# Attention, expert choice and feed-forward on one core: the first expert's number read at another place, and twelve products of the identity by itself

## The chip, the core and the metric

The kernel runs on one core of a Trainium2 chip. The metric is the device time of one launch in microseconds (us). Four engines compute: PE (TensorE, matrix products and transposes), DVE (VectorE), ACT (ScalarE) and POOL (GpSimd). SP (SyncE) issues most transfers, POOL the indirect ones that gather rows. All inputs and results are float32.

## What is computed

```python
def reference(**kwargs):
    attn_out = _attn_ref(q, k, v)                  # 2 x 12 heads, 448 tokens, head size 64, causal
    x = attn_out.transpose(0, 2, 1, 3).reshape(896, 768)
    x = _moe_ref(x, w_gate, w1, w2)
    return _moe2_ref(x, w_gate, w_val, w_out, rms_g)

def _moe_ref(x, w_gate, w1, w2):
    logits = x @ w_gate                            # 896 tokens, 8 experts, 112 tokens to each
    for idx in np.argsort(-logits.flatten()):      # greedy: best pair first
        tok, e = idx // E, idx % E
        if assigned[tok] >= 0 or counts[e] >= cap: continue
        assigned[tok] = e; counts[e] += 1
    for e in range(E):
        h = np.maximum(x[assigned == e] @ w1[e], 0.0)
        out[assigned == e] = h @ w2[e]
    return out

def _moe2_ref(x, w_gate, w_val, w_out, rms_g):
    xn = x / rms(x) * rms_g
    g = xn @ w_gate
    return silu(g) * (xn @ w_val) @ w_out
```

## The kernel before

It has three stages. Attention goes head by head and leaves its result in DRAM (`xs`, line 285) and the logits in `acc`. Then come eight rounds. In each, the fullest expert is found, the 112 tokens that it gets are named, their rows are gathered from `xs` into `xg`, and PE multiplies them with that expert's weights. The feed-forward stage follows.

The order of the work on PE, DVE, ACT and POOL is written out by hand, in strings of words that `emit` (line 710) turns into calls. A word with a prime belongs to the round before that of the same word without one. The string that the change touches is `START1`, which is run once, between attention and the first expert; in it a prime means round 0, no prime round 1, and a `+` work of the first expert. SP's order is not written out, it follows from the program.

Words of one round, as they stand in `START1`:

- `M`: the best logit of each token (`m`), which PE transposes into a row (`mr`, line 406) and ACT copies (`ms`, line 408).
- `G` and `P`: seven comparisons on DVE (`G`, lines 415 to 419; the second on POOL, all in four buffers in turn), and seven groups of seven small products on PE (`pc`, line 427: 8 columns each), which count for each token how many stand before it.
- `Q0`, `Q1`: the sums on PE (`ptot`, line 449), the choice of the expert on DVE (`kx`, line 476) and the tokens' places (`pos`, line 488).
- `Q2`: the expert's number as an integer (`eid`, line 492, one DVE instruction on one element), which SP reads into a register (line 493). The loads of the expert's 16 blocks of weights (`raw`, line 569, 384 KB each, on SP's queue) take their address from it.
- `O`, `F0`, `F1`: a table of places (line 497), seven products on PE (`pi`, line 505), the token numbers (`idx`, line 509), and the gather of 112 rows into `xg` (line 512, issued by POOL).
- `X0`, `X1`: PE transposes `xg` (`tp`, line 599), ACT copies it (`xf`, line 608). `U`, `D`: the expert's two products with the weights (`hp`, line 649, and `y`, line 663); the first `U` needs both copies and the first block of weights.

The `hp` sums lie in the accumulator banks of tag `c`, `cs` holds the identity (`ident`).

Of the kernel before, what the change touches and what calls it, by code (L numbers as in the profile page):

```python
# [24 lines left out]
F1 = 1024  # L25
# [11 lines left out]
SPLIT = 4  # L37
AHEAD = 18
START0 = 'M0 M1 G G'
START1 = "G1' G' P0' P1' G' P2' P3' P4' G' P5' G1' P6' Q0' Q1' M1 O' G F0' F1' G P0 P1 Q2' G G G P2 P3 G X0 P4 P5 G X1 P6 U0+ Q0 U1+ U2+ Q1 U3+ U4+ O"  # L40
ITER0 = "Y1 A0 M1 N2 U5 G F0' G U6 Q2' F1' U7 Y0 G G G D0 N1 P0 P1 A1 P2 D1 D2 D3 G P3 D4 G X0 D5 P4 P5 P6 N0 D6 Q0 X1 D7"
ITER = "U0 Q1' U1 N0 N1 N2 U2 U3 Q2' A0 M1 Y0 U4 O' Y1 G U5 F0' U6 F1' U7 A1 G D0 G P0 G P1 D1 D2 G P2 P3 G D3 D4 G D5 P4 P5 D6 P6 X0 D7 Q0 X1"
LASTR = "U0 C2 B4 U1 N0 N1 N2 I0 U2 U3 A0 Y0 Y1 U4 J2 B5 I1 U5 U6 C3 U7 D0 A1 J3 B6 D1 C4 B7 D2 D3 J4 C5 D4 J5 D5 C6 D6 D7 K0"
# [32 lines left out]
def tile_attn_moe_ffn(ctx, tc, qk, v, consts, wts, wgv, wout, rmsg, out):  # L76
    nc = tc.nc
# [9 lines left out]
    def banks(name, tag="c"):  # L87
        return pools["ps"].tile([128, 2, 512], F32, tag=tag, name=name, bufs=1)
# [4 lines left out]
    ident = cs[:, C_ID:C_ID + 128]  # L93
# [424 lines left out]
    def half64(src, j):  # L518
        return src[j // 4, j // 2 % 2, :, j % 2 * 384:j % 2 * 384 + 384]

    def load64(src):
        raw = ring.tile([128, 384, 2], U32, tag="raw", name="w64", bufs=NR)
        nc.sync.dma_start(out=raw, in_=src.bitcast(U32).rearrange("p (a b) -> p a b", b=2))
        return raw

    def widen(raw):
        g = cv.tile([128, 384], F32, tag="g64", name="g64", bufs=3)
        nc.scalar.activation(g, raw[:, :, 1].bitcast(F32), AF.Copy, scale=2.0 ** -112)  # L528
        gu = g.bitcast(U32)
        t = cv.tile([128, 384], U32, tag="t64", name="t64", bufs=3)  # L530
        x = t.bitcast(F32)
        nc.vector.tensor_scalar(t, gu, 3, None, op0=ALU.logical_shift_left)
        nc.vector.scalar_tensor_tensor(t, gu, 0x80000000, t, op0=ALU.bitwise_and, op1=ALU.bitwise_or)  # L533
        nc.vector.tensor_scalar(gu, t, 0xFF800000, None, op0=ALU.bitwise_and)
        nc.vector.scalar_tensor_tensor(g, raw[:, :, 0], 2.0 ** -52, g, op0=ALU.mult, op1=ALU.mult)  # L535
        nc.vector.tensor_add(x, x, g)  # L536
        return x

    def halves(x, hi, lo):
        nc.scalar.copy(hi, x)  # L540
        nc.vector.tensor_sub(lo, x, hi.bitcast(F32))
# [3 lines left out]
    def gate_val(half, which, dcs):  # L545
        c0 = half * S
        wh, wl = early[which]
        if (half, which) not in gv0:
            gv0[half, which] = bank("a" if half else "r", "pg")
        for dc in dcs:  # L550
            for n, (w, x) in enumerate(((wh, xnh), (wh, xnl), (wl, xnh))):
                nc.tensor.matmul(gv0[half, which][:, :S], w[:, dc * 128:dc * 128 + 128], x[:, dc, c0:c0 + S],  # L552
                                 start=(dc == 0 and n == 0), stop=(dc == 5 and n == 2))

    def tiles64():
        return (ring.tile([128, 768], F32R, tag="hi", name="hi", bufs=NH),
                ring.tile([128, 768], F32R, tag="lo", name="lo", bufs=NH))
# [135 lines left out]
    def turn_ids(c):  # L693
        if c == 0:
            nc.gpsimd.tensor_copy(idxf, idx)
            row = rt.tile([128, N], F32, tag="ms", name="ms", bufs=1)
            idrow.append(row[0:1])
            for half in range(2):
                pr = bank("r", "pr")
                for e in range(4):  # L700
                    nc.tensor.matmul(pr[0:1, e * CAP:e * CAP + CAP], idxf[:, 4 * half + e:4 * half + e + 1],
                                     ident[:CAP, :CAP], start=True, stop=True)
                nc.scalar.copy(idrow[0][:, half * 4 * CAP:(half + 1) * 4 * CAP], pr[0:1, :4 * CAP])
        else:
            pt = bank("r", "pt")
            for t in range(NT):
                nc.tensor.matmul(pt[:, t:t + 1], idrow[0][:, t * 128:t * 128 + 128], ones[0:1, 0:1], start=True, stop=True)
            nc.vector.tensor_copy(idt, pt[:, :NT])

    def emit(words, r0):  # L710
        for w in words.split():
            op, c, r = w[0], int(w[1:].rstrip("'+") or 0), r0 + w.count("+")
            if op in "MGPQ" or op in "OF":
                k = r + 2 - (w[-1] == "'")
                if 0 <= k < E:
                    getattr(rounds[k], op)(c)
            elif op == "K":
                half, which, part = c // 4, c // 2 % 2, c % 2
                gate_val(half, which, range(3 * part, 3 * part + 3))
            elif op == "S":  # L720
                sg0[c] = cv.tile([128, S], F32, tag="sg", name="sg", bufs=2)
                nc.scalar.activation(sg0[c], gv0[c, 0][:, :S], AF.Silu)
            elif op == "I":
                turn_ids(c)
            elif op == "B":
                raws64.append(load64(half64(wgv, c)))
            elif op == "C":
                wide.append(widen(raws64[c]))
            elif op == "J":
                if c % 2 == 0:  # L730
                    early.append(tiles64())
                hi, lo = early[c // 2]
                c0 = c % 2 * 384
                halves(wide[c], hi[:, c0:c0 + 384], lo[:, c0:c0 + 384])
            elif op == "X":
                if r + 1 < E:
                    if c == 0 and r >= 0:
                        exps.append(Expert(r + 1))
                    getattr(exps[r + 1], op)(c)
            elif op in "NY":  # L740
                if r > 0:
                    getattr(exps[r - 1], op)(c)
            else:
                getattr(exps[r], op)(c)

    ET = mybir.EngineType
    with tc.manual_schedule(engines={ET.PE, ET.Activation, ET.DVE, ET.Pool}):
        emit(START0, -2)
        emit(START1, -1)
        for r in range(E):  # L750
            emit(ITER0 if r == 0 else LASTR if r == E - 1 else ITER6 if r == E - 2 else ITER, r)
        emit(END, E)

    ectx.close()
    with ExitStack() as fctx:
# [13 lines left out]
        for fc in range(NFC):  # L769
            gh, gl = early[2 * fc] if fc < PRE else pair64(wgv[fc, 0])  # L770
            vh, vl = early[2 * fc + 1] if fc < PRE else pair64(wgv[fc, 1])
            for half in range(2):
# [3 lines left out]
                else:  # L776
                    pg = bank("a", "pg")
                    pv = bank("r", "pv")
                    for dst, wh, wl in ((pg, gh, gl), (pv, vh, vl)):
                        for dc in range(6):  # L780
                            for n, (w, x) in enumerate(((wh, xnh), (wh, xnl), (wl, xnh))):
                                nc.tensor.matmul(dst[:, :S], w[:, dc * 128:dc * 128 + 128], x[:, dc, c0:c0 + S],  # L782
                                                 start=(dc == 0 and n == 0), stop=(dc == 5 and n == 2))
# [112 lines left out]
```

## Time and profile before

| what | value |
|---|---|
| median of 3 runs | 613.68 us (613.35 to 613.87) |
| profiled execution, whole | 612.4 us |
| profiled execution, span from the first to the last instruction | 610.6 us |
| PE busy | 582.0 us, 95% of the span |
| DVE, ACT, POOL busy | 413.3, 231.3, 109.5 us |
| PE's share of the chain of work that ended last | 89% |
| gather `xg` and its share of that chain | 2% |
| mean clock granted to PE, of full speed | 0.976 |

The profile numbers its stretches in microseconds from the first instruction. Attention ends at about 119 us, the first `hp` product stands at about 141 us. A busy PE is one whose records cover the time; a granted clock of 1.00 is 2.4 GHz, 0.50 is 1.2 GHz.

### The profile page before, as it was taken

The page shows a single profiled execution, that of the slowest core. Times are in us where ns is not written, and L with a number is a line of the kernel's source. Part 1 is how long each engine was busy: PE and PEld are TensorE (multiplying, and loading weights), DVE is VectorE, ACT ScalarE, POOL GpSimd, SP SyncE. Part 2 cuts the span into 40 slices and gives each one's busy share as a digit, 9 for nine tenths or more (in the row PEclk, how much of TensorE's full clock was granted, in tenths as well). Part 3 has the DMA queues.
Part 4 walks back from the last instruction along what each step waited for, and adds up shares of the span by engine and source line. Part 5 has one row for each costly group of instructions (what it writes and reads, how often), then busy time and mean ns, then how long its engine had stood idle before and what let it go on. Part 6 is the DMA issues. An engine that isn't in the chain of part 4 may idle for free.

```text
span 610.6 us, 10757 instructions
## 1 busy us (share of the span) xinstructions
PE 582.0 (95%) x3814; PEld 518.9 (85%) x3814; DVE 413.3 (68%) x1176; ACT 231.3 (38%) x561; POOL 109.5 (18%) x102
## 2 busy tenths in 40 slices
PE   4899999758999999999999999999999999999995
PEld 3899999738697796877968799999999999999995
DVE  7799999695464454644364699999999972991400
ACT  5799999401031121120232444344343434331100
POOL 4677875130120201202000000000000000000210
PEclk9899999957999999999999999999999999999999
DMA  8988871109995958659794355445455530100210
GB/s 277 271 260 258 258 226 32 32 13 383 351 352 212 353 183 337 257 190 362 272 384 134 127 155 156 129 132 151 131 156 135 149 106 0 53 1 0 104 49 30
DMA packets 47973, 109.32 MB, mean 179 GB/s; under 512 B 15232, under 2 KB 17408, under 8 KB 47920
## 3 DMA queue, kind: packets, MB, share of 16 engines
q1 hardware_dynamic: 45280, 93.96, 47.2%
q0 software_dynamic: 2640, 14.68, 7.5%
q8 instruction: 30, 0.49, 0.3%
q14 instruction: 23, 0.19, 0.1%
HBM read 103.12 MB, written 5.51 MB: 178 GB/s over the span
## 4 chain that ended last, share of the span: by engine, by line
PE 89%; DMA 5%; issue 2%; DVE 2%; SPq 1%; ACT 1%; POOL 1%; POOLq 0%; ACTq 0%; DVEq 0%
PE hp L649 14%; PE pv L782 13%; PE pg L782 13%; PE y L663 13%; PE o L803 12%; PE sp L178 4%; PE ot L237 4%; PE pt L207 4%; PE pn L264 3%; PE pg L552 2%; DMA xg<-xs,idx 2%; DMA cs<-in_consts 2%; PE tp L599 2%; PE pc L427 1%; PE mr L406 1%
## 5 line engine op out<-in xcount | busy, mean ns | idle before, releaser
L649 PE MATMUL hp<-xf,raw 128*128 128x112 f32 x768 | 92.3, 279 | 0.1
L649 PEld LDWEIGHTS hp<-xf,raw 128*128 128x128 f32 x768 | 89.4, 194 | 1.7 <-ACT hf L652 0.5
L663 PE MATMUL y<-raw,hf 128*112 128x384 f32 x256 | 89.4, 491 | 0.0
L663 PEld LDWEIGHTS y<-raw,hf 128*112 128x112 f32 x256 | 42.6, 177 | 27.4
L810 POOL DMA_INDIRECT out<-ob,idt x7 | 6.8, 969 | 296.2 <-ACT ob L809 290.5
L540 ACT CAST hi<-t 128x384 fp32r<-128x384 f32 x58 | 29.7, 512 | 58.4 <-DVE t L536 56.4
L199 ACT ACTIVATE pe<-sm,nm 128x256 f32<-128x256 f32 (+3 forms) x84 | 48.6, 582 | 2.5 <-DVE nm L189 2.1
L512 POOL DMA_INDIRECT xg<-xs,idx x8 | 21.5, 2684 | 155.3 <-DVE G L415 134.2
L782 PE MATMUL pv<-xnh,hi 128*128 128x448 f32 x132 | 48.2, 365 | 0.0
L782 PE MATMUL pv<-xnh,lo 128*128 128x448 f32 x132 | 48.2, 365 | 0.0
L782 PE MATMUL pv<-xnl,hi 128*128 128x448 f32 x132 | 48.2, 365 | 0.0
L782 PE MATMUL pg<-xnh,hi 128*128 128x448 f32 x132 | 48.2, 365 | 0.0
L782 PE MATMUL pg<-xnl,hi 128*128 128x448 f32 x132 | 48.2, 365 | 0.0
L782 PE MATMUL pg<-xnh,lo 128*128 128x448 f32 x132 | 48.2, 365 | 0.0
L189 DVE CUSTOM_DVE_ANT_0 sm<-sp,mask 128x384 f32<-128x384 f32 (+3 forms) x84 | 42.1, 514 | 2.9 <-PE sp L178 2.1
L207 PE MATMUL pt<-cs,pe 128*128 128x128 f32 x228 | 40.8, 286 | 3.3 <-DVE ptl L224 2.8
L224 DVE TENSOR_TENSOR ptl<-pt,pth 128x512 fp32r<-128x512 f32 (+3 forms) x84 | 41.4, 514 | 2.5 <-ACT pth L220 2.5
L528 ACT ACTIVATE g<-w 128x384 f32<-128x384 f32 x72 | 39.8, 554 | 5.7 <-DVE t L536 5.7
L220 ACT CAST pth<-pt 128x512 fp32r<-128x512 f32 (+3 forms) x84 | 37.1, 444 | 9.9 <-PE pt L207 8.0
L533 DVE SCALAR_TENSOR_TENSOR t<-g,t 128x384 uint32<-128x384 uint32 x72 | 39.1, 552 | 0.3
L536 DVE TENSOR_TENSOR t<-t,g 128x384 f32<-128x384 f32 x72 | 39.1, 552 | 0.3
L535 DVE SCALAR_TENSOR_TENSOR g<-w,g 128x384 f32<-128x384 uint32 x72 | 39.0, 552 | 0.3
(153 smaller groups left out, 1217.1 us busy)
## 6 DMA issues: line engine op xcount, KB each, us to landing
raw<-in_wts SPq DMA_DIRECT2D x128, 384.0 KB, 7.5
w<-in_wgv SPq DMA_DIRECT2D x48, 384.0 KB, 3.3
w<-in_wout SPq DMA_DIRECT2D x24, 384.0 KB, 3.2
hi<-in_qk POOLq DMA_DIRECT2D x10, 896.0 KB, 6.3
qr<-in_qk SPq DMA_DIRECT2D x11, 448.0 KB, 5.5
vr<-in_v SPq DMA_DIRECT2D x12, 224.0 KB, 4.6
xs<-xl SPq DMA_DIRECT2D x12, 224.0 KB, 3.8
kr<-in_qk SPq DMA_DIRECT2D x10, 224.0 KB
```

Source lines behind the costliest of these rows:

```text
L189: nc.vector.tensor_tensor_reduce(out=sm[:, :w], in0=sp[:, :w], in1=mask[:, MOFF[t]:MOFF[t] + w], op0=ALU.add, op1=ALU.min, scale=-0.125, s ...
L199: nc.scalar.activation(pe[:, :w], sm[:, :w], AF.Exp, bias=nm[:, t:t + 1], scale=-1.0, accum_out=sums[:, t:t + 1])
L207: nc.tensor.transpose(pt[:, b * 128:b * 128 + 128], pe[:, b * 128:b * 128 + 128], ident)
L224: nc.vector.tensor_sub(*rest.pop((h, t)))
L528: nc.scalar.activation(g, raw[:, :, 1].bitcast(F32), AF.Copy, scale=2.0 ** -112)
L533: nc.vector.scalar_tensor_tensor(t, gu, 0x80000000, t, op0=ALU.bitwise_and, op1=ALU.bitwise_or)
L535: nc.vector.scalar_tensor_tensor(g, raw[:, :, 0], 2.0 ** -52, g, op0=ALU.mult, op1=ALU.mult)
L536: nc.vector.tensor_add(x, x, g)
L649: nc.tensor.matmul(o, w[:, dc * 128:dc * 128 + 128], self.x[0][:, dc, :], start=(dc == 0), stop=(dc == 5))
L663: nc.tensor.matmul(self.ys[:CAP, u, :SQ], a, b[:, u * SQ:u * SQ + SQ], start=(c == 0 and i == 0), stop=(c == 7 and i == len(ps) - 1))
L782: nc.tensor.matmul(dst[:, :S], w[:, dc * 128:dc * 128 + 128], x[:, dc, c0:c0 + S], start=(dc == 0 and n == 0), stop=(dc == 5 and n == 2))
L803: nc.tensor.matmul(o[u][:, :SQ], x[:, fc % 6, :], w[:, u * SQ:u * SQ + SQ], start=(fc == 0 and n == 0), stop=(fc == NFC - 1 and n == 2))
```

## The change

In `START1` the word `Q2'` moves: it stood after the first two `P` of round 1, it now stands right after `Q1'`, ahead of `M1` and `O'`. New words `W1`, `W2`, `W2`, `W2`, `W5` stand after `F1'`, after the `P0`, `P1` and `P2` of round 1, and after `P3`, right ahead of the first `X0`. A word `Wn` multiplies the identity by itself n times (float32, 128 by 128 with 128 columns) into a bank of tag `c`; nothing reads the result.

```diff
-START1 = "G1' G' P0' P1' G' P2' P3' P4' G' P5' G1' P6' Q0' Q1' M1 O' G F0' F1' G P0 P1 Q2' G G G P2 P3 G X0 P4 ...
+START1 = "G1' G' P0' P1' G' P2' P3' P4' G' P5' G1' P6' Q0' Q1' Q2' M1 O' G F0' F1' W1 G P0 W2 P1 W2 G G G P2 W2 P3 W5 G X0 P4 ...
@@ emit
+            elif op == "W":
+                warm = banks("warm")[:, 0, :128]
+                for _ in range(c):
+                    nc.tensor.matmul(warm, ident, ident, start=True, stop=True)
```

On DVE, before: the row of the chosen expert's table (`oh`) and what follows it in round 0, up to the expert's number.

```order
L396 TENSOR_TENSOR oh<-ohf,km 128x56
L497 TENSOR_TENSOR O<-iota,pos 128x784
L499 SCALAR_TENSOR_TENSOR gone<-eo,gone 128x8
L416 SCALAR_TENSOR_TENSOR G<-ms,m,cs 128x128
L419 TENSOR_SCALAR G<-ms,m 128x768
L509 TENSOR_SCALAR idx<-pi 112x1
L415 TENSOR_SCALAR G<-ms,m 128x128
L416 SCALAR_TENSOR_TENSOR G<-ms,m,cs 128x128
L419 TENSOR_SCALAR G<-ms,m 128x640
L492 TENSOR_SCALAR eid<-kx 1x1
```

On DVE, now, the same stretch from the same row:

```order
L396 TENSOR_TENSOR oh<-ohf,km 128x56
L492 TENSOR_SCALAR eid<-kx 1x1
L497 TENSOR_TENSOR O<-iota,pos 128x784
L499 SCALAR_TENSOR_TENSOR gone<-eo,gone 128x8
L416 SCALAR_TENSOR_TENSOR G<-ms,m,cs 128x128
L419 TENSOR_SCALAR G<-ms,m 128x768
L509 TENSOR_SCALAR idx<-pi 112x1
```

The expert's number has moved ahead of eight instructions, among them `O` and `idx`, on which the gather rests. SP's order of instructions is the same in both kernels: the reading of the number stood, and stands, right ahead of the 16 loads.

On PE, before: the end of `P3` of round 1, then the transposes of the gathered rows, then `P4`.

```order
L427 LDWEIGHTS G
L427 MATMUL pc<-oh,G 128x8
L599 MATMUL tp<-cs,xg 128x112 x6
L427 LDWEIGHTS G
L427 MATMUL pc<-oh,G 128x8
```

On PE, now, the same place:

```order
L427 LDWEIGHTS G
L427 MATMUL pc<-oh,G 128x8
L726 MATMUL warm<-cs 128x128 x5
L599 MATMUL tp<-cs,xg 128x112 x6
L427 LDWEIGHTS G
```

Five of the twelve products stand between `P3` and the transposes that wait for the gather; the other seven stand one and two at a time between `pi`, `P0`, `P1`, `P2` and `P3`. Nothing else changes its place on any engine.

## Rows read from the trace of the kernel before

**Rows 1.** The page's 40 slices of 15.3 us: granted clock in tenths.

```profile
PEclk9899999957999999999999999999999999999999
```

**Rows 2.** Chain of work that ended last, 130 to 170: start us, us, what.

```profile
130.72 1.10 PE mr L406 x4
...
134.03 5.03 DMA xg<-xs,idx
...
139.10 1.38 PE tp L599 x6
140.48 0.54 PE pc L427 x21
141.02 2.74 PE hp L649 x12
143.76 0.43 PE ptot L449 x2
144.19 5.39 PE hp L649 x48
...
153.07 9.13 DMA xg<-xs,idx
...
162.25 0.80 PE tp L599 x6
...
164.34 0.51 PE pc L427 x21
...
166.23 0.21 PE ptot L449 x2
```

**Rows 3.** Busy us (and instructions) by stretch, then granted clock, DMA share, GB/s.

```profile
118.00:122.00 4.00, 1.59 (x16) 1.19 (x15) 3.20 (x13) 0.97 (x2) 1.75 (x3) 0.78 0.26 57
...
143.00:144.00 1.00, 1.00 (x7) 1.00 (x6) 0.00 (x0) 0.00 (x0) 0.00 (x0) 0.50 1.01 406
144.00:146.00 2.00, 2.00 (x19) 2.00 (x19) 1.60 (x12) 0.00 (x0) 0.00 (x0) 0.98 1.03 410
```

**Rows 4.** Timeline of DVE: start us, us, line, operation, tiles, shapes, count.

```profile
131.50 0.97 DVE L497 TENSOR_TENSOR O<-iota,pos 128x784 bf16<-128x784 bf16 x1
...
132.99 0.62 DVE L419 TENSOR_SCALAR G<-ms,m 128x768 bf16<-128x768 f32 x1
133.53 0.22 DVE L509 TENSOR_SCALAR idx<-pi 112x1 uint32<-112x1 f32 x1
...
134.58 0.13 DVE L492 TENSOR_SCALAR eid<-kx 1x1 uint32<-1x1 f32 x1
```

**Rows 5.** SP's timeline from 130 to 170: the loads of weights from their first issue.

```profile
135.80 31.47 SPq L569 DMA_DIRECT2D raw<-in_wts  x32
```

**Rows 6.** SP's waits, 118 to 170: who for whom, total us, times, longest.

```profile
SPq L493 <- DVE G L415: 16.2, 1, 16.2
```

**Rows 7.** Transfers issued from 135 to 136: count, size, us from issue to landing.

```profile
raw<-in_wts SPq DMA_DIRECT2D x1, 384.0 KB, 4.2
```

**Rows 8.** POOL's timeline at the first two gathers.

```profile
134.03 1.72 POOL L512 DMA_INDIRECT xg<-xs,idx  x1 [7.34 <-DVE G L415]
153.07 2.38 POOL L512 DMA_INDIRECT xg<-xs,idx  x1 [17.32 <-DVE G L415]
```

**Rows 9.** The eight gathers of `xg`: us from issue to landing.

```profile
DMA to landing us min/median/max: 5.0/9.3/10.5
```

**Rows 10.** Queues, 136 to 137 (q0 gathers; q1, weights, none): packets, MB, share.

```profile
q0 software_dynamic: 16, 0.10, 65.6%
```

**Rows 11.** The same queues, 137 to 138.

```profile
q0 software_dynamic: 57, 0.24, 65.2%
```

**Rows 12.** The same queues, 157 to 158; q0 has no line in it.

```profile
q1 hardware_dynamic: 129, 0.35, 92.8%
```

**Rows 13.** The same queues, 158 to 159.

```profile
q0 software_dynamic: 34, 0.21, 64.4%
```

**Rows 14.** Timeline of PE: eight of the small products of round 1.

```profile
134.72 0.76 PE L427 MATMUL pc<-oh,G 128*128 128x8 bf16 x8 [0.28 <-DVE eid L492]
```

More of the change, by code (lines that the diff above doesn't have):

```diff
@@ L39 @@
 START0 = 'M0 M1 G G'
-START1 = "G1' G' P0' P1' G' P2' P3' P4' G' P5' G1' P6' Q0' Q1' M1 O' G F0' F1' G P0 P1 Q2' G G G P2 P3 G X0 P4 P5 G X1 P6 U0+ Q0 U1+ U2+ Q1 U3+ U4+ O"
+START1 = "G1' G' P0' P1' G' P2' P3' P4' G' P5' G1' P6' Q0' Q1' Q2' M1 O' G F0' F1' W1 G P0 W2 P1 W2 G G G P2 W2 P3 W5 G X0 P4 P5 G X1 P6 U0+ Q0 U1+ U2+ Q1 U3+ U4+ O"
 ITER0 = "Y1 A0 M1 N2 U5 G F0' G U6 Q2' F1' U7 Y0 G G G D0 N1 P0 P1 A1 P2 D1 D2 D3 G P3 D4 G X0 D5 P4 P5 P6 N0 D6 Q0 X1 D7"
```

## The prediction

> **What bounds the kernel now.** The chain of waits comes first: PE holds 89% of it, and the page's clock line shows one lasting dip below full speed, in slices 9 and 10, between attention and the first expert [rows 1]. Nothing else in the kernel is near this change, so the whole sum is made there. Read next is the chain through that stretch [rows 2]. The first gather, issued at 134.03, takes 5.03 us; at 139.10 PE starts on its rows, and from there PE has no gap until the second gather. So the gather's landing sets the start of everything behind it, and PE's clock sets the pace. The stretches say what that pace is [rows 3]: the clock falls in 118 to 122, where PE was busy for 1.59 of 4 us, it is 0.50 (1.2 GHz) until 144, after PE has run without a gap from 139.10, and 0.98 (practically 2.4 GHz) from 144 to 146. The first expert therefore starts at half clock, and its start costs tp 1.38, pc 0.54, hp 2.74 and ptot 0.43, together 5.09 us, up to 144.19.
>
> The same work at the upper level stands in the same view [rows 2]: tp 0.80, pc 0.51, ptot 0.21, and a block of hp at 5.39 x 12/48 = 1.35, together 2.87 us. **If the clock were up when the gathered rows come, 2.22 us would be won; if the rows come later, each microsecond is lost whole.** With x for the rows' arrival and S for the time of that work (2.87 to 5.09), the shift against now is x + S - 144.19. Behind it PE is the bound; the second gather and the second expert's weights hang on PE's and DVE's work in this start and shift with it.
>
> **The expert's number.** The eid instruction takes 0.13 us at 134.58 and goes to the place of O at 131.50 [rows 4], 3.08 us earlier. O, pi and the gather's idx stand behind it, at most 0.13 us later. This is covered: idx waits behind G of line 419 in DVE's row, which runs from 132.99 when ACT's copy is there, and O, which would end at 132.6 instead of 132.47, leaves pi the time to be done at about 133.5, before idx at 133.53. Without that cover it would cost 0.13. SP waited 16.2 us for nothing but this number [rows 6], so its first load, 135.80 now [rows 5], goes out at 135.80 - 3.08 = 132.72; the 16 loads follow on the same queue, all 3.08 us earlier. Does PE gain from that? The first block lands 4.2 us after issue, at 140.0 [rows 7], and hp begins at 141.02: the weights had a second to spare, and the blocks behind it run ahead of a PE that has no gaps. With a faster start (hp at 139.10 + 0.80 + 0.51 = 140.4) they still would be there. So the earlier weights are worth nothing by themselves.
>
> **What they do to the gather.** POOL has the first gather written out at 134.03 + 1.72 = 135.75 [rows 8], just as SP issues its first load. In 136 to 137 only gather packets move (16), in 137 to 138 there are 57 more, 73 of the some 80 [rows 10, 11]: the gather has the engines nearly to itself, and lands 5.03 us after issue, the least of the eight; the median is 9.3, the largest 10.5 [rows 9]. With the change, SP has been issuing for 3.03 us when POOL is done. The nearest row is the second gather: issued at 153.07, written out at 155.45, in a time when SP issues the second expert's weights. Its packets do not show until 158, the weights' queue moves 129 packets from 157 to 158 and the gather's none, then 34 of its packets go from 158 to 159 [rows 12, 13], and it lands at 162.20, 9.13 us after issue [rows 2]. Taking off what POOL needed more there, 2.38 - 1.72, gives 8.47 us, and **x = 134.03 + 8.47 = 142.50** instead of 139.06. The ends: 5.03 us, if nothing changes (139.06), and the largest, 10.5 (144.5). I take 142.5, since the second gather is the one that also enters behind loads begun shortly before, while the weights of the first expert lie there longer still.
>
> The Trainium skill, page "DMA: Bandwidth & Descriptors", section "Queues, rings and completion order", says that each DMA engine takes turns between the queues that have work, a packet from each. The trace doesn't bear it out for the start of the second gather, which sees none of its packets moved while the weights' queue moves 129 [rows 12], but does from 158 on [rows 13]; by that rule the time would be rival B's, 613.5.
>
> **The twelve products.** A product of 128 columns in float32 is two passes, as each of hp's six is (12 records for one block). At half clock hp takes 2.74/12 = 0.228 us a pass for 112 columns, so 0.261 for 128, 0.52 a product, 6.3 us for twelve; at the upper level 1.35/12 = 0.112, so 0.26 a product. They stand on PE in order, and tp, P4 to P6 and hp queue behind the last five. From pi's end at about 133.4 to tp at 139.10 there are 5.7 us; the 28 small products of P0 to P3 take 28 x 0.76/8 = 2.7 [rows 14], which leaves 3.0 us empty. At half clock throughout, the products would end at 133.4 + 2.7 + 6.3 = 142.4; up to that much is on the path if the gather comes at 139.06, and nothing of it if it comes at 142.5. DVE's comparisons reuse four buffers that P0 to P2 free, up to a microsecond later than now; P4 to P6, which need the last ones, come after the gather, which covers it.
>
> Do they bring the clock up? The one rise here comes after 5.0 us in which PE had no gap, 139.10 to 144.1. With the products PE has none to speak of from 130.72 on (mr, pi, then products and counts) [rows 2]. If mr and pi count, the rise is at about 135.7, else about 138.4. The rest then goes at twice the pace as far as the comparisons allow, and the products end between 139.0 and 140.4 (middle 139.7). **After that PE stands empty again until 142.5**, some 2 to 3.5 us, and it is after such a thin stretch (1.59 busy of 4) that the clock fell before. So S is between 2.87 (still up) and 5.09 (fallen, or never up). Nothing in the trace favours one, and I take the middle, 3.98.
>
> **The sum.** 142.50 + 3.98 - 144.19 = +2.3 us, with +1.2 to +3.4 for the two ends of S. The profiled execution would go from 612.4 to 614.7; it lies 1.3 under the median of the runs, which goes from 613.68 to 616.0. What the measurement can tell from no change is 0.2%, 1.23 us.
>
> **Rivals.**
>
> A, the forecast: the weights hold the gather up for longer than the clock gives back. For it: the median of the eight gathers is 9.3 us, and the first is the only one that meets no weights when it is written out. 614.9 to 617.1, at the largest landing of a gather 617 to 619.
>
> B, turns between the queues. The gather's packets took about two microseconds alone, 136 to 138 [rows 10, 11]; shared one to one they would take as long again: x = 139.06 + 2.0 = 141.1, after the products end, with the clock up: 141.1 + 2.87 - 144.19 = -0.2, so 613.5, no change. Against it stands the second gather's late start; for it, that the weights' packets begin some two microseconds after the first issue (135.80, and none before 137 [rows 10]), so at about 134.7 with the change, which leaves them a lead of only one over the end of POOL's work.
>
> C, the other side: the gather is not touched, or barely, and the products' clock decides. Then tp waits for the last product, at 139.7, and S is 2.87: 139.7 + 2.87 - 144.19 = -1.6, so 612.1, faster, at best -2.3 (611.4). It decides if the rows are there before about 140.1. This is also what comes out if the loads don't go out earlier, because something that the trace covers holds SP, so that the first half of the change does nothing.
>
> D, the products do nothing for the clock and stand in front of tp: with the gather at 139.06, tp starts at 142.4 and S is 5.09, +3.3, so 617.0. For it: the counts between them have only 8 columns, and where PE did them alone the clock stayed down. Against it: the rise at 144 came with just such matrix work as the products are.
>
> **How the numbers follow.** A 0.58, B 0.19, C 0.16, D 0.07. The likeliest is A, 616.0. The range leaves out C's better half (0.08) and the top of A (0.07): 612.1 to 617.8; A's own range is 614.9 to 617.1. Slower by over 0.2%: A but for its lowest end (0.51) and D, 0.58. Faster by over 0.2%: C but for its weak end, and a B with a little more clock, 0.18. Within 0.2%: B and the edges, 0.24.
>
> **What would show it.** Right: the first load issued at about 132.7; the gather issued at 134.0 and landing at 141 to 143, with weights' packets and none of its own just after 135.75; PE empty between the last product and tp; the granted clock up somewhere in 135.7 to 140, and down again, or mixed, in 142 to 147. Wrong: a landing before 140.5 (then B or C), or a clock that holds at the upper level through the gap and a landing near 141, which brings the sum to zero; or PE coming to tp later than the rows (D). If the second gather is no longer met by PE just as it lands (162.20 against tp at 162.25), the shift does not pass on whole, which I have assumed.

## The result: slower, and by more than forecast

| | before | after |
|---|---|---|
| median of 5 runs | 613.75 us (613.35 to 614.93) | 621.5 us (620.94 to 622.99) |
| ratio, 95% interval | | 1.013 [1.0112, 1.0149] |
| profiled execution, whole | 612.4 us | 621.5 us |
| its span | 610.6 us | 619.7 us |
| mean clock granted to PE | 0.976 | 0.971 |

The change costs 7.75 us by the medians. The forecast was slower, 616.0, with a range up to 617.8: the direction was right, the size was not, and the range did not hold the time.

In the two profiled executions the spans differ by 9.1 us. 1.9 of this is no effect of the change: `mr`, the first step behind attention, starts at 132.61 here and started at 130.72 before [rows 2], and the five run times of each kernel spread by 1.58 and 2.05 us. To compare kernels I therefore count from the start of `mr`.

The page's clock line of after has its dip in the same place as [rows 1], and it is deeper:

```profile
PEclk9999999855999999999999999999999999999999
```

The chain of work that ended last, of after (start us, us, what), against [rows 2]:

```profile
132.61 1.09 PE mr L406 x4
...
135.92 12.42 DMA xg<-xs,idx
148.38 1.38 PE tp L599 x6
149.77 0.54 PE pc L427 x21
150.31 2.74 PE hp L649 x12
153.05 0.43 PE ptot L449 x2
153.47 5.46 PE hp L649 x48
...
171.54 0.58 PE tp L599 x6
```

The first gather now takes 12.42 us instead of 5.03, which is 7.39 more. `tp` starts 15.77 us after `mr` instead of 8.38, `hp`'s block of 48 20.86 instead of 13.47: both 7.39 later. `tp` of the second gathered rows starts 38.93 after `mr` instead of 31.53, 7.40 later. The work between `tp` and that block takes 5.09 us, as before. So the whole loss is the one gather's, and it passes on undiminished.

POOL's timeline of after, the first two gathers, against [rows 8]:

```profile
135.92 5.12 POOL L512 DMA_INDIRECT xg<-xs,idx  x1 [7.34 <-DVE G L415]
162.44 2.38 POOL L512 DMA_INDIRECT xg<-xs,idx  x1 [21.40 <-DVE G L415]
```

POOL needs 5.12 us to write out the first gather, against 1.72 before: 3.40 more. From POOL's end (141.04) to the landing (148.34) it is 7.30 us, against 3.31: 3.99 more. Together that is the 7.39. The second gather's writing did not change.

SP's timeline and DVE's of after, against [rows 5] and [rows 4]:

```profile
134.61 41.99 SPq L569 DMA_DIRECT2D raw<-in_wts  x32
```

```profile
133.40 0.13 DVE L492 TENSOR_SCALAR eid<-kx 1x1 uint32<-1x1 f32 x1
133.46 0.95 DVE L497 TENSOR_TENSOR O<-iota,pos 128x784 bf16<-128x784 bf16 x1
...
135.42 0.22 DVE L509 TENSOR_SCALAR idx<-pi 112x1 uint32<-112x1 f32 x1
...
139.95 0.28 DVE L419 TENSOR_SCALAR G<-ms,m 128x128 bf16<-128x128 f32 x1
...
140.69 0.34 DVE L416 SCALAR_TENSOR_TENSOR G<-ms,m,cs 128x128 bf16<-128x128 f32 x1
```

The last line is the end of DVE's unbroken row of comparisons, 141.03, and POOL's writing ends with it, at 141.04. (In this round all seven comparisons run on DVE, the second too, each as up to three instructions, lines 415, 416 and 419.) Before, POOL was done at 135.75 while the comparisons went on for more than three microseconds.

The last comparison of that row before, in DVE's timeline of before:

```profile
138.85 0.33 DVE L416 SCALAR_TENSOR_TENSOR G<-ms,m,cs 128x128 bf16<-128x128 f32 x1
```

So the comparisons alone do not explain it. What stood among them before and does not now is the number's instruction, at 134.58, inside POOL's 134.03 to 135.75.

The kernel before had the slow writing too, in later gathers. POOL's timeline of before at the third and the last gather, then DVE's at the third, the last comparison ahead of an idle stretch:

```profile
177.94 3.29 POOL L512 DMA_INDIRECT xg<-xs,idx  x1 [22.48 <-DVE G L415]
...
302.56 0.92 POOL L512 DMA_INDIRECT xg<-xs,idx  x1 [21.09 <-DVE idx L509]
```

```profile
180.02 0.41 DVE L419 TENSOR_SCALAR G<-ms,m 128x384 bf16<-128x384 f32 x1
```

The third to the seventh gather take 3.29 us each, under comparisons; the last, with none beside it, takes 0.92. At the third, POOL is done at 181.23, 0.80 us after the comparisons' end at 180.43; at the second it is 0.81 us. So POOL still writes for some 0.8 us once DVE is free, and that it ends within 0.01 us of the row's end in after's first gather speaks against its having waited for that end.

The queues of after, 141 to 144 (first line) and 144 to 145 (q1 weights, q0 gathers: packets, MB, share), against [rows 10 to 13]:

```profile
q1 hardware_dynamic: 437, 1.20, 102.3%
...
q1 hardware_dynamic: 89, 0.25, 63.1%
q0 software_dynamic: 30, 0.18, 51.9%
```

For three microseconds after POOL is done, the weights' queue moves 437 packets and the gather's none.

Busy us (and instructions) of PE, PEld, DVE, ACT, POOL by stretch, then granted clock, DMA share and GB/s, of after:

```profile
138.00:140.00 2.00, 2.00 (x22) 1.88 (x21) 2.00 (x8) 0.00 (x0) 2.00 (x1) 0.50 0.94 210
...
144.00:146.00 2.00, 0.00 (x0) 0.00 (x0) 0.00 (x0) 0.00 (x0) 0.00 (x0) 0.50 1.04 332
...
152.00:154.00 2.00, 2.00 (x13) 2.00 (x13) 0.45 (x2) 0.00 (x0) 0.00 (x0) 0.61 1.03 399
```

PE is full while it does the products, its clock stays at 0.50 (1.2 GHz), then PE stands empty, and the clock rises only in 152 to 154. The end of the products and the start of `tp` in PE's timeline:

```profile
139.81 2.50 PE L726 MATMUL warm<-cs 128*128 128x128 f32 x10
148.38 1.38 PE L599 MATMUL tp<-cs,xg 112*128 112x112 f32 x6 [6.07 <-DMA xg<-xs,idx]
```

### The profile page after: what moved, and what is told of

Same layout as the page of the kernel before. It is cut to its first block, busy times and chain, and to the rows that moved or that the text cites. A ratio compares the mean times of both kernels' runs of the same rounds, so it can differ in the third digit from the quotient of the medians.

```text
span 619.7 us, 10804 instructions
## 1 busy us (share of the span) xinstructions
PE 588.8 (95%) x3838; PEld 525.8 (85%) x3838; DVE 413.8 (67%) x1176; ACT 231.5 (37%) x561; POOL 113.4 (18%) x102
## 4 chain that ended last, share of the span: by engine, by line
PE 90%; DMA 4%; issue 2%; DVE 2%; SPq 1%; POOL 1%; ACT 1%; POOLq 0%; ACTq 0%; DVEq 0%
PE hp L649 14%; PE y L663 14%; PE pv L786 13%; PE pg L786 13%; PE o L807 12%; PE sp L178 4%; PE pt L207 4%; PE ot L237 4%; PE pn L264 3%; PE pg L552 2%; DMA xg<-xs,idx 2%; DMA cs<-in_consts 2%; PE tp L599 1%; PE pc L427 1%; PE mr L406 1%
## 5 line engine op out<-in xcount | busy, mean ns | idle before, releaser
L512 POOL DMA_INDIRECT xg<-xs,idx x8 | 24.9, 3109 | 159.1 <-DVE G L415 138.0
```

## The experiments

**The theory** that the traces suggest: while DVE runs its comparisons back to back, POOL does not get to write the descriptions of the gather's transfers. The number's instruction, on one element, was the opening through which it got in; with it gone, POOL is kept out for most of the row. Then the gather also meets the weights, as forecast. **Rivals**: the weights' transfers slow down POOL's writing itself; or the products do something to the gather.

All edits are shown against the kernel before, the last two against the run ahead of them. A word `Zn` is n spare instructions of the number's own form on one element, read by nothing:

```diff
+        def spare(self):
+            sp = rt.tile([1, 1], U32, tag="spare", name="spare", bufs=1)
+            nc.vector.tensor_scalar(sp, self.kx[0:1], -1.0, float(E), op0=ALU.mult, op1=ALU.add)
```

The distances in this table are read from each kernel's POOL timeline and chain; the ratio has its 95% interval.

| kernel | POOL writes, us | POOL's end to landing | `tp` after `mr` | `hp` x48 after `mr` | ratio to before |
|---|---|---|---|---|---|
| before | 1.72 | 3.31 | 8.38 | 13.47 | 1 |
| after | 5.12 | 7.30 | 15.77 | 20.86 | 1.013 [1.0112, 1.0149] |
| number alone | 5.13 | 7.02 | 15.51 | 20.60 | 1.0121 [1.0084, 1.0157] |
| products alone | 1.72 | 3.5 | 9.65 | 12.72 | 0.9991 [0.997, 1.0013] |
| number late, weights late | 5.12 | 3.00 | 11.47 | 16.65 | 1.0039 [1.0015, 1.0063] |
| number early, spare in its place | 1.72 | 7.18 | 12.25 | 17.33 | 1.0082 [1.0053, 1.0112] |
| number early, spare two later | 3.40 | 7.87 | 14.63 | 19.72 | one run, 620.97 us |
| ten spares first | 1.06 | 2.9 | 7.64 | 13.56 | 1.002 [0.9989, 1.005] |
| ten spares, ten products | 1.06 | 2.9 | 9.96 | 12.78 | 0.9977 [0.9956, 0.9999] |
| 24 products | 1.73 | 3.1 | 11.03 | 13.86 | one run, 615.07 us |
| three spares, ten products | 1.16 | 2.9 | 8.80 | 12.10 | 0.9983 [0.9964, 1.0003] |
| one spare, ten products | 1.15 | 3.1 | 8.79 | 13.62 | 0.9976 [0.9958, 0.9994] |

### The number alone, the products alone

```diff
-START1 = "... Q0' Q1' M1 O' G F0' F1' G P0 P1 Q2' G G G P2 ...
+START1 = "... Q0' Q1' Q2' M1 O' G F0' F1' G P0 P1 G G G P2 ...
```

> The number read early, no products. Theory T: the gather alone makes the loss, in two parts. POOL's writing of it stretches from 1.72 to about 5.1 us, because DVE's row of comparisons has no more opening once the number's instruction has left it; and then the written gather stands behind the weights, 7.3 instead of 3.3 us to landing. Then this kernel lands the gather 12.4 us after issue, tp starts some 7.4 us later than in the kernel before, and the time is 7 to 8 us above it, about 621. Rival P: the products have a part in it (they keep PE, and with it the comparisons' buffers, busy). Then the gather lands by 143 and the time is 616 or less. The clock is at the lower level until about 5 us after tp in both.

POOL's timeline and the chain of the number alone:

```profile
134.76 5.13 POOL L512 DMA_INDIRECT xg<-xs,idx  x1 [7.33 <-DVE G L415]
```

```profile
134.76 12.15 DMA xg<-xs,idx
146.96 1.38 PE tp L599 x6
```

Median 620.64 us. The number's place makes nearly the whole loss, 7.13 of the 7.39 us at `hp`'s block, 5.13 us of writing included. The products have hardly a part in it: with them `hp`'s block is 0.26 us later than without, and the ratio's interval with them lies inside the one without.

```diff
-START1 = "... F0' F1' G P0 P1 Q2' G G G P2 P3 G X0 ...
+START1 = "... F0' F1' W1 G P0 W2 P1 W2 Q2' G G G P2 W2 P3 W5 G X0 ...
```

> The twelve products, the number read at its old place. Theory T: POOL writes in 1.7 us, the gather lands 5.0 us after issue, as before; the products end some 3 us after that (they took 6.7 us with the counts between them at the lower clock), tp waits for them, and the clock is still at the lower level: +3.0 us, about 616.7. If the clock rises by the products after all: between -1.6 and +0.5 us. Rival P: POOL's writing is stretched here too, and the loss is near that of the whole change.

PE's busy time and clock of the products alone, by stretch (columns as above):

```profile
142.00:143.00 1.00, 1.00 (x7) 1.00 (x7) 0.00 (x0) 0.00 (x0) 0.00 (x0) 0.50 0.96 337
143.00:144.00 1.00, 1.00 (x27) 0.99 (x25) 0.00 (x0) 0.69 (x2) 0.00 (x0) 0.98 0.99 381
```

Median 613.58 us, ratio 0.9991: no change, and not the 616.7 that I expected. In this execution the clock is up before `hp`, during `tp`, some 10 us after `mr`, where before it rose at 144, some 13 after. But the products stand in front of `tp`, which starts 9.65 us after `mr` instead of 8.38. 1.27 lost against 5.09 - 3.07 = 2.02 won leaves 0.75 in the profiled execution; the ratio's interval, 0.997 to 1.0013, holds both that and no gain at all.

### The number late: no opening, and no weights either

```diff
-START1 = "... G P0 P1 Q2' G G G P2 P3 G X0 P4 P5 G X1 P6 ...
+START1 = "... G P0 P1 G G G P2 P3 G X0 P4 P5 G Q2' X1 P6 ...
```

The number is read after the last comparison, so the loads go out later than before, and not earlier.

> The number read later than before, behind the last comparison, so that it leaves DVE's row but the weights do not come early. Theory T: POOL's writing takes about 5.1 us although no weights move, and the gather lands 3.3 us after that, 8.4 us after issue. Rival Q: POOL writes in 1.7 us and the gather lands 5.0 us after issue. The time is above the one before in both, since the first block of weights now lands some 4.6 us later, at about 144.6 on the clock of the kernel before, and hp waits for it: +3.6 us, about 617.3.

POOL's timeline, then DVE's, then the chain:

```profile
135.89 5.12 POOL L512 DMA_INDIRECT xg<-xs,idx  x1 [7.33 <-DVE G L415]
```

```profile
140.66 0.34 DVE L416 SCALAR_TENSOR_TENSOR G<-ms,m,cs 128x128 bf16<-128x128 f32 x1
140.92 0.14 DVE L492 TENSOR_SCALAR eid<-kx 1x1 uint32<-1x1 f32 x1
```

```profile
135.89 8.12 DMA xg<-xs,idx
144.06 1.38 PE tp L599 x6
```

POOL's writing again takes 5.12 us and ends with the comparisons (141.01 and 141.00), though no weights move: the rival that the weights slow POOL falls. From POOL's end to the landing it is 3.00 us, against 3.31 in before: this gather meets no weights when it is written. The time is 617.21 us, ratio 1.0039, near the 617.3 that I expected, but not for the reason that I gave: `hp` does not wait for the late weights, it starts 1.92 us after `tp`, as before. So the two halves of the loss come apart: without the weights' half, `hp`'s block starts 3.18 us later than before.

### The number early, with a spare in its old place, and two comparisons later

```diff
-START1 = "... Q0' Q1' M1 O' G F0' F1' G P0 P1 Q2' G G G P2 ...
+START1 = "... Q0' Q1' Q2' M1 O' G F0' F1' G P0 P1 Z1 G G G P2 ...
```

> The number read early, no products, and a spare instruction of the same kind (one element of kx, read by nothing) at the number's old place in DVE's row. Theory T: the opening is back, POOL writes in about 1.7 us; what is left is the queue of weights: landing 8 to 9 us after issue, +3.0 to +4.0 us, about 617. Rival Q: it is the weights' transfers that slow POOL's writing as well; then POOL takes about 5 us here too and the time is that of the number alone.

With the spare in the number's old place, POOL's timeline, then DVE's, then the chain:

```profile
135.32 1.72 POOL L516 DMA_INDIRECT xg<-xs,idx  x1 [7.33 <-DVE G L415]
```

```profile
135.87 0.13 DVE L497 TENSOR_SCALAR spare<-kx 1x1 uint32<-1x1 f32 x1
```

```profile
135.32 8.90 DMA xg<-xs,idx
144.26 1.38 PE tp L603 x6
```

One instruction that nothing reads brings POOL back to 1.72 us. What is left is the weights' half: landing 8.90 us after issue, `hp`'s block 3.86 us later than before, 618.84 us at the median, where I had about 617. 3.86 and the 3.18 of the last run add up to 7.04, against the 7.13 of the number alone.

The spare in the other place, two comparisons (six instructions) later:

```diff
-START1 = "... Q0' Q1' M1 O' G F0' F1' G P0 P1 Q2' G G G P2 ...
+START1 = "... Q0' Q1' Q2' M1 O' G F0' F1' G P0 P1 G G Z1 G P2 ...
```

> The number read early, no products, the spare instruction two comparisons later in DVE's row than where the number stood. Theory T (an instruction on DVE that leaves POOL an opening sets when the gather is written out): POOL ends about 1.9 us later than with the spare at the old place, so it takes about 3.6 us instead of 1.72, and the gather lands 10.5 to 11 us after issue instead of 8.9. If the place of the opening does not matter, POOL takes 1.7 or 5.1 us.

POOL's timeline and DVE's:

```profile
136.32 3.40 POOL L516 DMA_INDIRECT xg<-xs,idx  x1 [7.33 <-DVE G L415]
```

```profile
138.71 0.13 DVE L497 TENSOR_SCALAR spare<-kx 1x1 uint32<-1x1 f32 x1
```

The spare's place sets POOL's end: 139.72, 1.01 us after the spare's start, where it was 137.04, 1.17 after, with the spare in the old place, and 135.75, 1.17 after the number, in the kernel before. The landing came 11.27 us after issue, a little past the 10.5 to 11 that I expected. With these two runs it is shown, and not only argued, that such an instruction lets POOL in. What in it does so is not: the spares differ from a comparison in size, in the type that they write and in what they read, and no run separates these.

Where POOL got in when there was no spare is open as well. From the end of the spare or the number's instruction to POOL's end it is 0.88 to 1.04 us in these runs and in before. In after POOL ends 0.81 us behind line 419's instruction of 128 columns, which ends at 140.23, and in the number late and the number alone it is 0.80 and 0.81 behind the same instruction. The equal distances speak for its having got in there, but no run moved that instruction.

### Ten spares ahead of the comparisons

```diff
-START1 = "... O' G F0' F1' G P0 P1 Q2' ...
+START1 = "... O' G F0' F1' Z10 G P0 P1 Q2' ...
```

> The kernel before with ten spare instructions of one element on DVE right behind idx, so that the opening is there when POOL begins; the number where it was, no products. Theory T: POOL writes in about 0.9 us, as it does for the last gather where DVE has no comparisons, the gather lands about 4.2 us after issue instead of 5.0, the comparisons end 0.6 us later, and tp starts 0.8 us earlier: -0.6 to -0.8 us against the kernel before, about 0.1%. If T is wrong: POOL stays at 1.7 us or more and the time is the same or 0.6 us longer.

DVE's timeline and POOL's:

```profile
136.04 1.71 DVE L497 TENSOR_SCALAR spare<-kx 1x1 uint32<-1x1 f32 x10
```

```profile
136.41 1.06 POOL L516 DMA_INDIRECT xg<-xs,idx  x1 [7.33 <-DVE spare L497]
```

With DVE free of comparisons during the whole writing, it takes 1.06 us. So even in the kernel before some 0.66 us of the 1.72 went into waiting for the opening. `tp` starts 0.74 earlier after `mr`. But each spare took 0.17 us, 1.71 in all, the comparisons end later, and the small products that count them come to hold `hp` (its first twelve start at 143.46 here, 10.36 after `mr`; before it was 10.30). The gain that I expected, 0.6 to 0.8 us, is given back: ratio 1.002, no change. The profiled execution of this kernel took 621.05 us, where the median of the twelve is 615.1; the rows of the start are all that is read from it.

### Twice the products

```diff
-START1 = "... F0' F1' G P0 P1 Q2' G G G P2 P3 G X0 ...
+START1 = "... F0' F1' W2 G P0 W4 P1 W4 Q2' G G G P2 W4 P3 W10 G X0 ...
```

> Twenty-four products, two for each of the twelve, the number at its old place. If dense products bring the clock up: it rises before tp, somewhere among the last ten, the products end 12.5 to 14.5 us after the start of mr, and tp to ptot takes 2.9 us instead of 5.1: +1 to +3 us against the kernel before. If products of the identity don't count for the clock: it stays at the lower level to the end of them, 16 us after the start of mr, and for 3 to 5 us of the expert's work, +7 to +8 us.

Stretches and chain:

```profile
139.00:140.00 1.00, 1.00 (x11) 1.00 (x9) 1.00 (x4) 0.00 (x0) 0.00 (x0) 0.75 0.69 215
```

```profile
141.75 2.40 PE warm L726 x20
144.14 0.58 PE tp L599 x6
```

With 24 products the clock rises within 139 to 140, before `tp`, and before any work of the expert. So here it rose on the products and the counts between them alone. They end 11.03 us after `mr`, sooner than the 12.5 to 14.5 that I expected, but `tp` could start 8.38 after it, and the block of 48 starts 0.39 us later than before.

### Spares and products together

```diff
-START1 = "... F0' F1' G P0 P1 Q2' G G G P2 P3 G X0 ...
+START1 = "... F0' F1' Z10 W1 G P0 W2 P1 W2 Q2' G G G P2 W2 P3 W3 G X0 ...
```

> The ten spares behind idx, the number where it was, and ten products (1, 2, 2, 2 and 3 instead of 5 at the end). Theory T: the gather lands at 4.2 us, the products end about 1 us earlier than the twelve did, some 8.6 us after the start of mr, tp follows them; -0.5 to -1.5 us if the clock rises at the latest during tp as it did with the twelve, +0.5 us if it doesn't.

612.99 us, ratio 0.9977 [0.9956, 0.9999]: a little faster than both kernels, against before by a step that is hardly above what can be told. `tp` starts 9.96 us after `mr`, where I had the products end at 8.6: the ten spares stand on its chain with 0.15 us each.

The same with three spares, and with one:

```diff
-... F0' F1' Z10 W1 G P0 W2 P1 W2 Q2' ...
+... F0' F1' Z3 W1 G P0 W2 P1 W2 Q2' ...
+... F0' F1' Z1 W1 G P0 W2 P1 W2 Q2' ...
```

> The kernel before, with three one-element spare instructions (read by nothing) on VectorE right behind the gather's idx, ten identity products on TensorE, and the number at its old place. My theory: POOL needs an opening in VectorE's row only to get in, so three spares do what ten did: the gather's writing takes 1.06 to 1.3 us instead of 1.72, its landing comes 0.4 to 0.7 us sooner after idx than before, and the comparisons lose 0.5 us instead of 1.7, so they no longer stand on the chain. hp's block of 48 would start 12.0 to 12.6 us after mr (before 13.47, ten spares with products 12.78), and the time would be 0.3 to 0.7 us under the run with ten spares, about 612.3 to 612.7. Rival: POOL needs the comparisons out of the way for the whole of its writing; then three spares that end 0.5 us after idx leave the writing near 1.7 us, and the time is that of the products alone, no change against before (ratio 0.999).

> As the run with three spares, with one. My theory: if POOL is let in by whichever one-element instruction ends after POOL has the gather to write (0.28 us after idx in the trace of before), a single spare that ends before that does nothing, and the writing stays at about 1.7 us, set by the number's instruction three comparisons later; time as the products alone, ratio 0.999. Rival: POOL needs only a short gap anywhere near idx; then one spare is as good as three, the writing is 1.1 us and the time 0.2 us under that with three spares.

Three spares, POOL's timeline, then DVE's, then a stretch:

```profile
134.29 1.16 POOL L516 DMA_INDIRECT xg<-xs,idx  x1 [7.34 <-DVE spare L497]
```

```profile
133.93 0.48 DVE L497 TENSOR_SCALAR spare<-kx 1x1 uint32<-1x1 f32 x3
```

```profile
140.00:142.00 2.00, 2.00 (x32) 1.96 (x31) 0.54 (x5) 0.78 (x2) 0.00 (x0) 0.73 0.95 243
```

One spare, the same views:

```profile
136.48 1.15 POOL L516 DMA_INDIRECT xg<-xs,idx  x1 [7.33 <-DVE G L415]
```

```profile
136.12 0.13 DVE L497 TENSOR_SCALAR spare<-kx 1x1 uint32<-1x1 f32 x1
```

```profile
146.00:148.00 2.00, 2.00 (x14) 2.00 (x14) 1.02 (x8) 0.00 (x0) 0.00 (x0) 0.68 1.02 401
```

Three spares do for the writing nearly what ten did, as I expected, and `hp`'s block starts 12.10 us after `mr`, the earliest of all. For one spare my expectation was wrong: it ends at 136.25, before POOL's row even begins, and yet the writing takes 1.15 us and not 1.7. Its end lies 1.38 us ahead of POOL's, 137.63, further than the 0.88 to 1.04 of the runs above; whether POOL got in by it or by something behind it, and at what moment POOL wants in, the rows do not show, and this stays open. In time the two don't differ: 614.2 and 613.82 us, ratios 0.9983 and 0.9976; for three spares I had expected 612.3 to 612.7. The interval of the products alone overlaps with all three kernels that have both, so that the spares add anything to the time is not shown. What does differ is the clock of the two profiled executions. PE's work is the same in both, without a gap from `pi` on; with three spares the clock rises in 140 to 142, some 10 us after `mr`, with one spare in 146 to 148, some 14 after it. On that hang the 1.5 us between 12.10 and 13.62.

## Why the prediction was half right

**What bounds the kernel: right.** The landing of the first gather set the start of everything behind it, and the shift passed on whole. That the direction came out is no luck: 3.99 of the 7.39 us are the weights' half, which the forecast had.

**The number, the loads: right.** SP's first load went out at 134.61; less the 1.89 us by which attention ended later, that is 132.72, as forecast. `O` and `idx` lost nothing: 135.42 less 1.89 is the 133.53 of [rows 4].

**The step that failed: "Taking off what POOL needed more there, 2.38 - 1.72, gives 8.47 us".** It takes POOL's 1.72 us of writing as given and puts the moved instruction's part in it at nothing. In fact the moved instruction was what made it 1.72. [Rows 4] and [rows 8] had it in sight: the number at 134.58 lay inside POOL's 134.03 to 135.75, the only instruction on one element in a row of comparisons. I had costed what that instruction takes, 0.13 us, and what waits for its result, and not what its being there lets others do. Without it POOL writes 5.12 us: +3.40. That the third to the seventh gather were written in 3.29 us under comparisons, and the last in 0.92 without, stood in the same trace. The upper end of the range from [rows 9], 10.5, was no bound either: POOL wrote none of the eight gathers of before for longer than 3.29 us.

**The weights in front of the gather: right.** With POOL at 1.72 us the landing took 8.90 us after issue, where I had 8.47 from the second gather. After itself shows the same share: 7.30 us from POOL's end, against 8.47 - 1.72 = 6.75, +0.55. Of the packets forecast for the weights and none for the gather, [rows 12, 13], the trace of after shows 437 to 0. Rival B, turns from the start, did not happen.

**The products: the clock wrong, the empty PE right but too short.** They ended at 142.31, in before's time 140.4, the end of what I had forecast with a rise of the clock; without one I had 142.4. The difference is in the 28 small products between them, which take 0.17 us for seven in the chain of the products alone, 0.7 in all, and not 2.7. PE then stood empty, for 6.07 us instead of some 2 to 3.5. And the clock did not rise, neither at 135.7 nor at 138.4 in before's time. The work from `tp` to `ptot` took 5.09 us, the end of S and not the middle of 3.98: +1.11.

**The sum, closed.** The forecast's terms give 142.50 + 3.98 - 144.19 = 2.29; the 0.04 us between landing and `tp`, which it left out, makes that 2.33. 2.33 + 3.40 (POOL's writing) + 0.55 (its packets behind the weights) + 1.11 (S) = 7.39 us, which is what the trace has at `hp`'s block; the medians have 7.75.

**The rivals.** A was the mechanism, with one term missing. C needed the rows before 140.1 and D the products in front of `tp`; neither came about. Products in front of `tp` are what the products alone and the 24 show, there with the clock up.

The Trainium skill, page "SBUF — State Buffer", section "🔬 SBUF: two separate sides", has a box on this: a DMA that GpSimd issues has its descriptors written by GpSimd, and while VectorE runs an instruction in a two-port mode, GpSimd is locked out of the port pair that they share and can't write them. The trace agrees in that the writing takes 5.12 us under the comparisons and 1.06 beside spares. I had not weighed it. The Trainium skill, same page, section "Who interferes with whom", says that whoever issues first holds the pair for the whole instruction. Here POOL was held up for more than one instruction: from 136.00 to 139.95 twelve instructions of the comparisons followed each other, and POOL was done only at 141.04, where one instruction on a single element had let it finish within 1.17 us. Which mode each comparison ran in, no row here shows.

## What to carry to other kernels

Before moving a small instruction, look at what the other engines do while it runs: a step that costs 0.13 us may be the gap in which POOL writes a gather. Where an indirect transfer is issued under a long unbroken row of VectorE work, compare POOL's row for that issue with one issued while VectorE rests; if it is several times longer, try one cheap instruction in the row, close behind the indices: here it gave back 3.41 of 5.13 us of writing. It pays only if the writing is on the critical path; ten such instructions by themselves left the time of this kernel as it was. And bulk loads that are sent out before a gather on the critical path cost it some four microseconds here, so earlier is not better for a transfer that has slack.

## What the runs showed of the hardware

- POOL's issue of the same 112-row gather took 1.06 us beside spares, 1.15 and 1.16 with one and three of them ahead, 1.72 with one opening 0.55 us after its start, 3.40 with the opening at 2.39, and 5.12 to 5.13 with none under a row that ran on beside it to its end.
- From POOL's end, the first gather landed after 2.9 to 3.5 us where the first load of weights was issued after it, and after 7.0 to 7.9 where the loads had been going out for 3.0 to 6.4 us.
- PE's clock: a full PE does not fix the moment at which it rises. In after PE was busy from `pi` at 134.50 to 142.3, and the granted clock stayed at 0.50; with 24 products it rose within 139 to 140; with the same ten products it rose 10 us after `mr` in one execution and 14 in another. What decides between them, the runs don't settle.
- Ten one-element instructions of VectorE that write the same tile took 0.17 us each, 1.71 together; with 0.13 us for one by itself, they held up the comparisons by more than the 0.6 us that I had allowed for.
